# A gated linear recurrence with two dense blocks on one core: transfers issued some chain steps later, and a triangular solve laid out evenly over the chain

## The chip, the cores and the metric

The kernel runs on 1 core of one Trainium2 chip. The metric is the device time of one execution in microseconds (us); lower is better. The time before is a median of 1053.01 us over 2 runs (1050.19 and 1055.84).

## The reference, cut to what matters

Three blocks follow each other. The first, on which the change works, is a delta-rule recurrence over 768 positions with a 48 x 48 state for each of 4 x 8 (batch, head) pairs; two dense blocks in fp32 accuracy come after it.

```
k_n = k / (norm(k) + 1e-6)
for t in range(S):
    y[:, :, t] = q[:, :, t] @ state
    v_old = state^T k_n[t]
    state = state + beta[t] * outer(k_n[t], v[t] - v_old)
x = y as (4, 768, 384)
x = x + (gelu(x w_in)[u] * (w_sg layernorm(gelu(x w_in)[v]) + b)) w_out      # first dense block
x = u + relu(u w_ch1) w_ch2,   u = x + (relu(x^T w_tok1) w_tok2)^T           # second dense block
```

## The kernel before, in words

The recurrence (phase_a) is computed in chunks. The work is cut into 6 groups: 2 halves of the batch times 3 spans of 256 positions. For each group five things happen.

- **kk** (PE, lines 130 to 156): products of the keys (tile kq) with themselves, 4 units per group. ACT copies each unit into the staging tile gf, of which there is one buffer for two units; after the second and the fourth unit, six transfers within SBUF put gf into md and G (lines 152 and 153).
- **solve** (DVE, lines 158 to 195): a transpose of md into Li (line 161), a square root on ACT, eleven small steps of preparation, then 31 pairs, a product p (line 186) and a sum into T (line 188), each pair on the result of the last: the substitution. Then T is transposed into md (line 191) and into Tn (line 194). tload issues four transfers from md into tw (line 204).
- **merge** (PE, ACT; lines 209 to 242): 8 steps of products on tw, the first of them at line 216.
- **qk** (PE, DVE; lines 115 to 127): products of the keys with the queries (tile aq), 4 units; DVE masks each into aq (line 126).
- **chain** (PE, ACT; lines 248 to 303): 4 chunks of 4 steps (u, d0, y0, y1), 16 steps in all, which carry the state S from chunk to chunk through PSUM and the tiles yr. POOL multiplies the values v into yr (vput, line 247). The chains of the six groups run one after the other.

Every engine runs its instructions in the order in which the program emits them; nothing is reordered. The order is written by hand: while chain g emits its 16 steps, a table (ACT, one row per chain, one entry per step) says what is emitted behind each step: Q a unit of qk of group g+1, K a unit of kk of group g+3 (in chain 0 also of group 2), m a step of merge of group g+1, S n steps of the solve at hand, l the load of v, v a vput, z a memset of part of tw, c a piece of the conversion of the first dense block's weights (DVE lines 412 to 417, POOL, ACT), which goes on beside chains 1 and 2. A step S of the kind "pair" emits one pair. Between the two instructions of a pair a function (filler, line 317) may emit one step of the next group's solve, whenever that group's four units of kk have been emitted; it does so at a rate of 0.4 a call.

All loads go through SyncE's queue (SP), in the order of emission, as do the transfers within SBUF. A transfer that has to wait for the last reader of its buffer holds all that stand behind it. kq has two buffers (line 65, 2 transfers of 256 KB a load); its next load is emitted right behind the last product that reads the buffer. At the end of chain g the load of kn for group g+2 is emitted (line 83, 2 x 384 KB), and right behind it, as chain g+1 begins, those of bt for group g+3 (line 88, 16 KB) and of the queries for group g+2 (line 76, 2 x 512 KB). v is line 80.

In chain 5 the dense part begins beside the chain, and from there to the end PE multiplies.

Of the kernel before, what the change touches and what calls it, by code (L numbers as in the profile page):

```python
# [29 lines left out]
def phase_a(tc,I,xn,cfg,tail=None,beside=None,room=None):  # L30
    nc=cfg.get('wrap',lambda x:x)(tc.nc)
    es=ExitStack(); esE=ExitStack(); esP=ExitStack()
    with es:
# [80 lines left out]
        for par in range(2): nc.gpsimd.memset(AQs[1][T_[par],:,:,par].rearrange("p h b a c x -> p (h b) (a c x)"),0.0)  # L114
        def qk(g):
            for u in range(4):
# [6 lines left out]
                if u%2: load_kq()  # L123
# [4 lines left out]
        def kk(g):  # L128

            assert g<2 or merged[g-2]>=4 and loaded[g-2]  # L130
            for u in range(4):
# [7 lines left out]
                if u%2: load_kq()  # L139
# [6 lines left out]
                else:  # L146
                    if bb==0: gf=P1.tile([128,2,2,8,32],F32,name="gf")
                    nc.scalar.copy(gf[:,:,bb],gp.rearrange("p n (c i) -> p c n i",i=32))
                    if bb==1:
                        for r in range(4):  # L150
                            q=slice(32*r,32*r+32)
                            nc.sync.dma_start(md[q].rearrange("p (b h n) i -> p h b (n i)",b=2,h=2)[:,h],gf[q,r%2].rearrange("p b n i -> p b (n i)"))  # L152
                            if r%2==0: nc.sync.dma_start(G21[q].rearrange("p (b h n) i -> p h b (n i)",b=2,h=2)[:,h],gf[q,1].rearrange("p b n i -> p b (n i)"))
                done[g]+=1
                yield 'kk'
        done=[0]*6; merged=[0]*6; loaded=[0]*6; solved=[0]*6
# [160 lines left out]
        def filler():  # L317

            if len(run)>1 and done[run[1][0]]==4:
                acc[0]+=rate  # L320
                if acc[0]>=1: acc[0]-=1; next(run[1][1],None)
        def adv(n):
            for _ in range(n):
                if not run: return
# [10 lines left out]
        for ns in range(31):  # L335
            if ns==8: load_q(1); load_k(1)
# [4 lines left out]
        for k_ in range(4):  # L341
            many(s0,1)
            many(qks,1)
        many(ms,1); adv(1)
        many(ms,1)
        for k_ in range(6): many(ms,1); adv(1)
        vput(0,0)
        act=cfg['act']
        for g in range(6):
            if g+2<6: load_b(g+2)  # L350
            if g+1<6 and g>0: load_q(g+1)
# [4 lines left out]
            if g==5 and tail is not None:  # L356
                esP.close(); esE.close()
                fill=tail()
            for si,_ in enumerate(chain(g)):
                if fill is not None: next(fill,0)  # L360
                for a in act[min(g,5)][si].split():
# [7 lines left out]
                    if a=='l' and g<5: load_v(g+1)  # L369
# [3 lines left out]
            if g+2<6: load_k(g+2)  # L373
# [354 lines left out]
_mid=['m z S3','m S3','S3','S3','S3','Q S3','Q S3','Q S3','Q S3','l m S2','m S2','m S2','m K S2','m K S2','m K S2','K v S2']  # L728
_c=lambda row,at:[a+' c' if i in at else a for i,a in enumerate(row)]
ACT=[['S4 K','S4 K','S4 K','S4 K','S4','Q S4','Q S4','Q S4','Q S4','l m S2','m S2','m S2','m K S2','m K S2','m K S2','K v S2'],  # L730
# [34 lines left out]
```

## Time and profile before

| | |
|---|---|
| median of 2 runs | 1053.01 us |
| the profiled execution's own time | 1051.51 us |
| its span, first to last instruction | 1049.8 us |
| busy: PE, DVE, ACT, POOL | 872.0, 627.5, 350.7, 282.5 us |
| mean granted clock of PE | 0.904 of full speed |
| chains 0 to 4 (start of chain 0 to start of chain 5) | 76.2 to 366.6 us |

The profile is one execution. Its span is cut by stage: the first 76 us are the first loads, kk and the solve of group 0; then chains 0 to 4; then chain 5 beside the dense part. Group g's merge and chain need group g's solve, and a chain's middle needs the queries of the next group. A wait in brackets behind a row is idle time of that engine, put down to what came last.

### The profile page before, as it was taken

Reading aid. Unit: us, or ns where it says so; the run is one execution under the profiler, and the core shown is the slowest. Engines: PE = TensorE matmul, PEld = TensorE weight load, DVE = VectorE, ACT = ScalarE, POOL = GpSimd, SP = SyncE. Lnnn points to the kernel's source line nnn. Section 1 sums busy time; section 2 is a strip of 40 time slices with the busy share of each in tenths; the row PEclk is TensorE's granted clock in tenths of the full one; section 3 lists DMA queues with packets and bytes.
Section 4 is the critical chain, followed back from the end, with each engine's and each line's share of the span. In section 5 each row is a group of like instructions: output and inputs, shape, how many; then the busy total and the mean of one; then the engine's idle time right before and its main releaser. Section 6 shows DMA issues by size and latency. Waiting matters only on the chain.

```text
span 1049.8 us, 23037 instructions
## 1 busy us (share of the span) xinstructions
PE 872.0 (83%) x9644; PEld 827.4 (79%) x9644; DVE 627.5 (60%) x1294; ACT 350.7 (33%) x809; POOL 282.5 (27%) x358
## 2 busy tenths in 40 slices
PE   6375455755566998999999999789999999999998
PEld 4165455645556877899999999778889999999998
DVE  7977919969584247887494789786942222222222
ACT  2042233443326576444242343343422112112111
POOL 8110121645403143432232344482420000000000
PEclk7588678866778899999999999898999999999999
DMA  7633355573545143200000002222400000000000
GB/s 182 140 64 93 71 144 114 155 168 111 133 109 109 31 137 118 64 1 2 1 1 1 1 11 81 70 85 68 133 31 23 2 23 23 1 23 23 1 23 23
DMA packets 60024, 68.05 MB, mean 65 GB/s; under 512 B 30224, under 2 KB 37136, under 8 KB 59920
## 3 DMA queue, kind: packets, MB, share of 16 engines
q1 hardware_dynamic: 57808, 60.28, 21.8%
q0 software_dynamic: 2112, 6.29, 1.9%
q8 instruction: 76, 1.25, 0.5%
q14 instruction: 28, 0.23, 0.1%
HBM read 51.61 MB, written 7.86 MB: 57 GB/s over the span
## 4 chain that ended last, share of the span: by engine, by line
PE 60%; DVE 18%; ACT 7%; DMA 5%; issue 5%; SPq 4%; POOL 1%; DVEq 0%; ACTq 0%; POOLq 0%
PE ps L488 17%; PE ps L489 17%; PE ps L490 17%; DVE T L188 3%; DVE p L186 2%; DMA md<-gf 2%; DVE F L412 2%; DMA aq<-in_qt_dram 2%; DVE F L413 2%; PE gm L122 2%; PE gm L226 2%; SPq L152 2%; DVE aq L126 1%; PE gm L216 1%; PE ps L512 1%
## 5 line engine op out<-in xcount | busy, mean ns | idle before, releaser
L580 DVE SCALAR_TENSOR_TENSOR hlo<-ps,hh 128x384 fp32r<-128x384 f32 x96 | 53.5, 557 | 207.4 <-ACT hh L579 207.4
L579 ACT ACTIVATE hh<-ps 128x384 fp32r<-128x384 f32 x96 | 47.2, 492 | 228.2 <-PE ps L490 228.2
L488 PE MATMUL ps<-GU,SB 128*128 128x384 f32 x288 | 98.2, 341 | 0.0
L490 PE MATMUL ps<-GU,SB 128*128 128x384 f32 x288 | 98.0, 340 | 0.0
L489 PE MATMUL ps<-GU,SB 128*128 128x384 f32 x288 | 97.7, 339 | 0.0
L247 POOL TENSOR_TENSOR yr<-v,nn 64x192 f32<-64x192 f32 x96 | 50.9, 530 | 161.4 <-PE yp L255 84.8
L186 DVE TENSOR_TENSOR p<-Li,T 128x31 f32<-128x31 f32 (+15 forms) x186 | 71.2, 385 | 5.6
L122 PE MATMUL gm<-aq,kq 128*64 128x64 f32 x768 | 39.2, 270 | 41.0 <-issue 26.2
L188 DVE TENSOR_TENSOR T<-T,p 128x112 f32<-128x112 f32 (+15 forms) x186 | 69.4, 375 | 5.8
L122 PEld LDWEIGHTS gm<-aq,kq 128*64 128x64 f32 x768 | 35.7, 182 | 43.5 <-issue 35.6
L489 PE MATMUL ps<-SB,VHt 128*128 128x384 f32 x192 | 65.6, 342 | 2.3 <-POOL SB L390 2.3
L490 PE MATMUL ps<-VHt,hlo 128*128 128x384 f32 x192 | 65.3, 340 | 1.3 <-DVE hlo L580 1.3
L488 PE MATMUL ps<-SB,VHt 128*128 128x384 f32 x192 | 65.6, 341 | 0.0
L490 PE MATMUL ps<-SB,VHt 128*128 128x384 f32 x192 | 65.1, 339 | 0.0
L488 PE MATMUL ps<-VHt,hh 128*128 128x384 f32 x192 | 65.0, 338 | 0.0
L489 PE MATMUL ps<-VHt,hh 128*128 128x384 f32 x192 | 64.6, 337 | 0.0
L489 PEld LDWEIGHTS ps<-GU,SB 128*128 128x128 f32 x288 | 54.5, 189 | 0.7 <-DVE GU L505 0.7
L488 PEld LDWEIGHTS ps<-GU,SB 128*128 128x128 f32 x288 | 54.6, 190 | 0.5 <-DVE GU L505 0.5
L555 POOL TENSOR_TENSOR q<-q,u 128x384 f32<-128x384 f32 x32 | 36.9, 1156 | 66.4 <-DVE q L554 66.4
L490 PEld LDWEIGHTS ps<-GU,SB 128*128 128x128 f32 x288 | 54.4, 189 | 0.3 <-POOL SB L390 0.3
L488 PE MATMUL ps<-X,SA 128*128 128x384 f32 x144 | 50.0, 347 | 5.6 <-DVE xn L567 3.1
L265 PE MATMUL Sps<-yr,kn 128*48 128x48 f32 x704 | 31.6, 232 | 27.1 <-ACT yr L281 13.8
(157 smaller groups left out, 2313.9 us busy)
## 6 DMA issues: line engine op xcount, KB each, us to landing
kq<-in_kq_dram SPq DMA_DIRECT2D x48, 256.0 KB, 4.3
st<-in_ch_dram SPq DMA_DIRECT2D x36, 256.0 KB, 2.8
aq<-in_qt_dram SPq DMA_DIRECT2D x12, 512.0 KB, 8.0
v<-in_vn_dram SPq DMA_DIRECT2D x12, 384.0 KB, 5.6
kn<-in_kn_dram SPq DMA_DIRECT2D x12, 384.0 KB, 6.8
out_dram<-xn SPq DMA_DIRECT2D x24, 192.0 KB, 1.9
tw<-md SPq DMA_DIRECT2D x24, 128.0 KB, 3.7
st<-in_win_dram POOLq DMA_DIRECT2D x12, 256.0 KB, 4.0
```

The source lines that it names most:

```text
L122: nc.tensor.matmul(gp[T_[par],n,:],kq[F_,par,64*n:64*n+64],aq[F_,par,n//2,n%2,:],start=True,stop=True)
L152: nc.sync.dma_start(md[q].rearrange("p (b h n) i -> p h b (n i)",b=2,h=2)[:,h],gf[q,r%2].rearrange("p b n i -> p b (n i)"))
L186: nc.vector.tensor_tensor(p,Li[:,j,j+1:].unsqueeze(1).to_broadcast([128,w,n]),T[:,:w,j].unsqueeze(2).to_broadcast([128,w,n]),ALU.mult)
L188: nc.vector.tensor_tensor(T[:,:w,j+1:],T[:,:w,j+1:],p,ALU.add)
L247: n0=8*h+cc; nc.gpsimd.tensor_tensor(YRs[bb][gc%3][T_[par],:,par,:],VS[bb][T_[par],n0:n0+7:2,:],NNs[g%3][T_[par],16*bb+n0:16*bb+n0+7:2].un ...
L265: nc.tensor.matmul(Sps[bb][D_[par],pair,:],KNs[pb][F_,bb,par,c,pair,:],yr[F_,pair,par,:],start=(gc==0 and pair==0 and bb==0),stop=True,ski ...
L488: nc.tensor.matmul(ps,L[0],Rr[0],start=first,stop=False)
L489: nc.tensor.matmul(ps,L[0],Rr[1],start=False,stop=False)
L490: nc.tensor.matmul(ps,L[1],Rr[0],start=False,stop=last)
L555: nc.gpsimd.tensor_tensor(gt,gt,u2[:,d,t],ALU.mult)
L579: nc.scalar.activation(hi,ps,AF.Relu)
L580: nc.vector.scalar_tensor_tensor(lo,ps,0.0,R(hi),op0=ALU.max,op1=ALU.subtract)
```

## The change

Line numbers of the new kernel are some 10 higher (L152 is L161, L161 is L171, L186 is L196, L191 is L201, L126 is L134).

Three things are done. First, transfers are not emitted at once but put on a list (later) and emitted a number of chain steps on (tick counts them down at each step): kq 2 steps later, the md and G transfers 1 step later, bt and the queries at the first step of the chain, kn at the third (and only behind the queries), v 2 steps later. Second, the filler may begin a solve only 8 chain steps behind its last unit of kk. Third, the table gives each chain 38 solve steps, 2 or 3 at each chain step, which is one solve to a chain; chains 0 and 4 have 4 a step until the solve at hand is done. The second half of solve 5 so moves into chain 4, whose merge steps begin one step later.

```diff
+        wait=[]
+        def later(fn,n=cfg['late']):
+            wait.append([n,fn])
+        def tick():
+            for w in list(wait):
+                w[0]-=1
+                if w[0]<=0: wait.remove(w); w[1]()
...
-                if u%2: load_kq()
+                if u%2: later(load_kq)
...
                     if bb==1:
-                        for r in range(4):
-                            q=slice(32*r,32*r+32)
-                            nc.sync.dma_start(md[q]...,gf[q,r%2]...)
-                            if r%2==0: nc.sync.dma_start(G21[q]...,gf[q,1]...)
-                done[g]+=1
+                        def out(h=h,gf=gf,md=md,G21=G21):
+                            ...
+                        later(out,1)
+                done[g]+=1; dat[g]=step[0]
...
-            if len(run)>1 and done[run[1][0]]==4:
+            if len(run)>1 and done[run[1][0]]==4 and step[0]>=dat[run[1][0]]+cfg['far']:
...
-                if not run: return
+                if not run or done[run[0][0]]<4: return
...
         for g in range(6):
-            if g+2<6: load_b(g+2)
-            if g+1<6 and g>0: load_q(g+1)
+            if g+2<6: later(lambda g=g:load_b(g+2),1)
+            if g+1<6 and g>0: later(lambda g=g:load_q(g+1),1)
+            if g and g+1<6: later(lambda g=g:load_k(g+1),3)
...
+                while wait: tick()
...
             for si,_ in enumerate(chain(g)):
+                step[0]+=1; tick()
...
-                    if a=='l' and g<5: load_v(g+1)
+                    if a=='l' and g<5: later(lambda g=g:load_v(g+1),2)
...
-            if g+2<6: load_k(g+2)
...
-_mid=['m z S3','m S3','S3','S3','S3','Q S3','Q S3','Q S3','Q S3','l m S2','m S2','m S2','m K S2','m K S2','m K S2','K v S2']
+_st=[2,3,2,3,2,2,3,2,2,3,2,2,3,2,2,3]
+_s=dict(m=(0,1,9,10,11,12,13,14),Q=(5,6,7,8),l=(9,),v=(15,))
...
-CFG={...,'rate':.4,'act':ACT}
+CFG={...,'rate':.4,'late':2,'far':8,'act':ACT}
```

How the instructions of two engines move, each time without the row numbers. First SyncE's queue in chain 1, around the first of the two sets of six md and G transfers of a group (md_142 and G_128 are those of group 4; kq_110 and kq_111 are the two key buffers). Before:

```order
L65 DMA kq_110<-in_kq_dram 64x2x512 x2
L152 DMA md_142<-gf 32x2x256
L153 DMA G_128<-gf 32x2x256
L152 DMA md_142<-gf 32x2x256 x2
L153 DMA G_128<-gf 32x2x256
L152 DMA md_142<-gf 32x2x256
L65 DMA kq_111<-in_kq_dram 64x2x512 x2
```

and after:

```order
L161 DMA md_142<-gf 32x2x256
L162 DMA G_128<-gf 32x2x256
L161 DMA md_142<-gf 32x2x256 x2
L162 DMA G_128<-gf 32x2x256
L161 DMA md_142<-gf 32x2x256
L65 DMA kq_110<-in_kq_dram 64x2x512 x2
```

The load of kq_110 stood ahead of the first set of six transfers and now stands behind it, so that it is what the second set follows; the load of kq_111 moved on likewise, behind the second set.

SyncE's queue a little later, where chain 2 starts, from the last two of the second set on (kn_101, bt_122, aq_97 are the loads for the next groups, tw_99 takes the result of solve 3). Before:

```order
L153 DMA G_128<-gf 32x2x256
L152 DMA md_142<-gf 32x2x256
L83 DMA kn_101<-in_kn_dram 64x2x768 x2
L88 DMA bt_122<-in_bt_dram 128x32
L76 DMA aq_97<-in_qt_dram 64x4x512 x2
L204 DMA tw_99<-md_143 32x32x32 x4
```

and after:

```order
L162 DMA G_128<-gf 32x2x256
L161 DMA md_142<-gf 32x2x256
L88 DMA bt_122<-in_bt_dram 128x32
L76 DMA aq_97<-in_qt_dram 64x4x512 x2
L65 DMA kq_111<-in_kq_dram 64x2x512 x2
L83 DMA kn_101<-in_kn_dram 64x2x768 x2
L214 DMA tw_99<-md_143 32x32x32 x4
```

The queries (aq) moved ahead of kn, and the second load of kq went between the two.

DVE at the end of solve 3 (T_147, p_154; Li_144 and md_142 belong to solve 4, md_143 and Tn_149 to solve 3; F is the weight conversion, aq_97 the masking of the next group's queries). Before:

```order
L186 TENSOR_TENSOR p_154<-Li_145,T_147 128x60
L188 TENSOR_TENSOR T_147<-T_147,p_154 128x30x2
L186 TENSOR_TENSOR p_154<-Li_145,T_147 128x31
L161 STREAM_TRANSPOSE Li_144<-md_142 128x1024
L188 TENSOR_TENSOR T_147<-T_147,p_154 128x31
L191 STREAM_TRANSPOSE md_143<-T_147 128x32x32
L194 STREAM_TRANSPOSE Tn_149<-T_147 128x32x32
L169 TENSOR_SCALAR rc<-sh 128x32
```

and after:

```order
L196 TENSOR_TENSOR p_154<-Li_145,T_147 128x60
L198 TENSOR_TENSOR T_147<-T_147,p_154 128x30x2
L196 TENSOR_TENSOR p_154<-Li_145,T_147 128x31
L198 TENSOR_TENSOR T_147<-T_147,p_154 128x31
L201 STREAM_TRANSPOSE md_143<-T_147 128x32x32
L134 TENSOR_TENSOR aq_97<-gm,mask 64x512 x2
L204 STREAM_TRANSPOSE Tn_149<-T_147 128x32x32
L171 STREAM_TRANSPOSE Li_144<-md_142 128x1024
L134 TENSOR_TENSOR aq_97<-gm,mask 64x512 x2
L425 TENSOR_SCALAR F<-st 128x256 x2
L426 SCALAR_TENSOR_TENSOR F<-st,F 128x256 x2
L427 SCALAR_TENSOR_TENSOR F<-st,F 128x256 x2
```

The transpose into Li_144 stood ahead of the last T of solve 3 and ahead of the transpose into md_143; now it stands behind both transposes of solve 3. The end of solve 3, which stood at the start of chain 2, now stands between the maskings of chain 2's steps 6 and 8.

## Rows read from the trace of the kernel before

**Rows 1.** The busy time of each engine in 13 stretches of the run, us from the span's start, from chain 0's start to chain 5's start. Columns: stretch, its length; then for PE, PEld, DVE, ACT and POOL the busy us (and the number of instructions); the granted clock of PE; the mean busy share of the DMA engines; GB/s moved.

```profile
76.17:120.04 43.87, 20.06 (x490) 19.20 (x485) 35.61 (x88) 10.95 (x31) 2.07 (x4) 0.76 0.29 66
120.04:148.75 28.71, 21.06 (x645) 19.90 (x647) 12.00 (x28) 13.39 (x29) 11.77 (x19) 0.80 0.55 137
148.75:163.41 14.66, 8.21 (x162) 7.60 (x158) 8.79 (x23) 6.44 (x19) 1.88 (x2) 0.60 0.69 155
163.41:183.65 20.24, 8.73 (x222) 8.34 (x223) 19.29 (x51) 3.89 (x13) 2.64 (x5) 0.83 0.43 97
183.65:211.70 28.05, 19.91 (x647) 18.62 (x649) 26.12 (x57) 14.83 (x34) 17.56 (x31) 0.81 0.49 145
211.70:229.99 18.29, 8.64 (x162) 8.32 (x158) 9.69 (x17) 7.52 (x21) 7.00 (x13) 0.63 0.86 195
229.99:251.87 21.88, 9.64 (x223) 9.28 (x224) 20.76 (x53) 3.65 (x11) 9.48 (x17) 0.62 0.45 119
251.87:276.36 24.49, 19.13 (x631) 18.12 (x632) 21.46 (x44) 12.95 (x27) 16.93 (x32) 0.85 0.43 129
276.36:296.21 19.85, 8.30 (x144) 7.45 (x140) 6.93 (x21) 6.77 (x19) 1.64 (x4) 0.59 0.70 141
296.21:312.75 16.54, 9.98 (x222) 9.70 (x223) 15.45 (x35) 2.87 (x9) 1.06 (x2) 0.77 0.19 59
312.75:327.60 14.85, 13.38 (x478) 12.51 (x479) 13.92 (x30) 10.25 (x23) 5.69 (x9) 0.89 0.22 65
327.60:349.49 21.89, 13.66 (x343) 12.99 (x341) 3.73 (x5) 8.47 (x24) 4.29 (x9) 0.77 0.64 128
349.49:366.60 17.11, 16.40 (x626) 15.64 (x625) 2.75 (x4) 13.45 (x31) 2.28 (x5) 1.00 0.09 28
```

**Rows 2.** Waits over the whole run: who waited for whom, us in total, times, the longest.

```profile
DVE Li L161 <- DMA md<-gf: 43.5, 4, 21.2
...
ACT gf L148 <- DMA md<-gf: 36.8, 5, 8.7
```

**Rows 3.** DVE in order of time at the start of chain 2. Columns here and in the groups of single instructions below: start us, us, engine, line, operation, out<-in, shapes, count, and in brackets the idle time before it with what ended it. The last two rows are the first of solve 4's preparation and its first product.

```profile
220.75 1.90 DVE L161 STREAM_TRANSPOSE Li<-md 128x1024 f32<-128x1024 f32 x1 [8.31 <-DMA md<-gf]
...
222.78 2.09 DVE L191 STREAM_TRANSPOSE md<-T 128x1024 f32<-128x1024 f32 x1
...
226.51 0.17 DVE L169 TENSOR_SCALAR rc<-sh 128x32 f32<-128x32 f32 x1
...
229.86 0.19 DVE L186 TENSOR_TENSOR p<-Li,T 128x31 f32<-128x31 f32 x1
```

**Rows 4.** SyncE's queue at the same place: issues of transfers.

```profile
197.09 1.31 SPq L65 DMA_DIRECT2D kq<-in_kq_dram  x2
198.45 1.19 SPq L152 DMA_DIRECT2D md<-gf  x1
...
216.99 1.24 SPq L83 DMA_DIRECT2D kn<-in_kn_dram  x2
...
218.91 1.24 SPq L76 DMA_DIRECT2D aq<-in_qt_dram  x2
```

**Rows 5.** DVE in chain 0: the transpose into Li of solve 2, and the md transpose of solve 1.

```profile
95.87 1.91 DVE L161 STREAM_TRANSPOSE Li<-md 128x1024 f32<-128x1024 f32 x1 [6.11 <-DMA md<-gf]
...
112.81 1.97 DVE L191 STREAM_TRANSPOSE md<-T 128x1024 f32<-128x1024 f32 x1
```

**Rows 6.** PE: the first merge product of group 1 in chain 0, and 32 query products of chain 2.

```profile
120.04 1.92 PE L216 MATMUL gm<-tw,G 128*32 128x32 f32 x62 [1.89 <-DMA tw<-md]
...
240.95 1.97 PE L122 MATMUL gm<-aq,kq 128*64 128x64 f32 x32 [7.59 <-issue]
```

**Rows 7.** ACT: the copy into gf that is the first of a group's second half, in chains 0, 1 and 2.

```profile
146.27 0.58 ACT L148 COPY gf<-gm 128x512 f32<-128x512 f32 x1 [7.88 <-DMA md<-gf]
...
208.57 0.59 ACT L148 COPY gf<-gm 128x512 f32<-128x512 f32 x1 [8.72 <-DMA md<-gf]
...
274.52 0.58 ACT L148 COPY gf<-gm 128x512 f32<-128x512 f32 x1 [6.28 <-DMA md<-gf]
```

**Rows 8.** The chain that ended last, in order of time: three pieces that are transfers under way. Columns: start us (the issue), us until landed, what.

```profile
85.49 2.05 DMA md<-gf
...
155.20 8.07 DMA aq<-in_qt_dram
...
202.28 6.20 DMA md<-gf
```

**Rows 9.** DVE, single instructions: the first of a weight conversion (line 412) and the product that follows the conversion; a T beside work of POOL; a masking; the first p of solve 5, a T of the same shape without work of POOL, and the solve's last T.

```profile
231.28 0.49 DVE L412 TENSOR_SCALAR F<-st 128x256 int32<-128x256 int32 x2
...
233.69 0.27 DVE L186 TENSOR_TENSOR p<-Li,T 128x112 f32<-128x112 f32 x1
...
236.80 0.77 DVE L188 TENSOR_TENSOR T<-T,p 128x175 f32<-128x175 f32 x1
...
239.45 1.39 DVE L126 TENSOR_TENSOR aq<-gm,mask 64x512 f32<-64x512 f32 x2
...
294.04 0.19 DVE L186 TENSOR_TENSOR p<-Li,T 128x31 f32<-128x31 f32 x1
...
320.13 0.34 DVE L188 TENSOR_TENSOR T<-T,p 128x175 f32<-128x175 f32 x1
...
324.34 0.21 DVE L188 TENSOR_TENSOR T<-T,p 128x31 f32<-128x31 f32 x1
```

## What I predict, and why

> **What bounds the kernel now.** I read the trace from the end. Of the span of 1049.8 us only the first third can move: from 366.6 us on chain 5 and the dense layers run, which the change does not touch. So I cut the stretch from chain 0's start (76.17) to chain 5's start (366.60) into stages, one row each [rows 1]. Three kinds recur. A runs from a group's last gf copy to the first product that needs the next queries (tile aq). B runs from there to the first merge product, line 216. C runs from that to the next group's last gf copy. The 13 rows add to 290.4 us, and in them DVE is busy for 196.5, PE for 177.1. Nothing is full over the whole; the engines take turns.
>
> Then the waits say who holds whom [rows 2]. DVE stands 43.5 us, four times, at the transpose into Li (line 161) for the transfers md<-gf. ACT stands 36.8 us because gf has one buffer and its next copy needs those transfers landed. Chain 2's start shows it in single rows [rows 3]: the Li transpose of solve 4 begins at 220.75 after 8.31 us of idleness, and the final md transpose of solve 3, ready since the last product p, comes behind it at 222.78. A helper that should fill gaps put the next solve's first step ahead of the last steps of the current one. SP shows why the transfer is late [rows 4]: two kq loads (256 KB each) go at 197.09, ahead of the md transfers at 198.45; and kn (2 x 384 KB) at 216.99 goes ahead of the queries at 218.91.
>
> **Part 1: the filler no longer starts a solve early.** In the order after, Li stands behind the md transpose of the solve before. In chain 0 the md transpose begins at 112.81 [rows 5]. Ahead of it go away: the wait 6.11, the transpose 1.90, the preparation of solve 2 (226.51 to 229.86 for solve 4 [rows 3], so 3.35) and some 1.0 of its first pairs, 12.4 in all. I give 1.5 back, since the masking products on DVE then wait for PE. The transfer to tw and its landing stay: from the transpose's end (114.8) to the merge at 120.04 [rows 6] are 5.2. So the first stage goes from 43.87 to 33.0.
>
> **Part 2: md<-gf before kq.** In C the second gf copy waits 7.88, 8.72 and 6.28 us [rows 7]. With SP free, six issues take 4.1 us (198.45 is the first, 202.28 the last, which is under way from then [rows 4, 8]); from the last one's issue to the landing it took 2.05 at best and 6.20 with kq under way [rows 8]. From the copy's end to the last landing that is some 5.7, of which ACT works 1.9 on merge copies (in between now too), so it waits 3.8. The saving is 4.1, 4.9 and 2.5: C becomes 24.6, 23.1 and 22.0. Bounds: if transfers still land as at 202.28, nothing is saved; if ACT waits for nothing, 7.9, 8.7 and 6.3.
>
> **Part 3: kn behind the queries.** After: md 4.1, bt 0.65, then aq, first issue 4.75 after the gf copy. Two transfers of 512 KB at the 195 GB/s with a 0.86 share [rows 1], so some 215 at full share, take 4.9, and 2.05 is added as for the smallest landing: A = 11.6. Before, it was 14.66, 18.29 and 19.85. I let the queries set A in each chain, since the rows of A end at the product that waited for them. The observed landing of 8.07 with kn ahead [rows 8] is the other end: A = 13.4. The Trainium skill, DMA: Bandwidth & Descriptors, section "Anatomy of one DMA", gives some 2.0 us plus the bytes at 436 GB/s; by it A would be 9.2 and the total 7 us lower. It speaks of transfers issued by GpSimd, these go through SP, and no row here shows such a rate.
>
> **Part 4: the solve ends just in time.** This is what the change pays. Before, solves 2 to 5 were complete one half chain before their merge. Now the md transpose stands at step 6 and the merge at step 9, so B is a chain of its own: products 2.0 at the low clock [rows 6], mask 1.4 [rows 9], two pairs 1.2, mask 1.4, two pairs 0.9, transpose 2.05, tw 5.2: 14.2. (A pair is a p and a T; 31 of them take 294.04 to 324.55 less four maskings, 24.9, or 0.80 each [rows 9], the last ones least.) In chains 1 and 2 a conversion of weights (231.28 to 233.69, 2.4, taken as 2.7 with its neighbour's start [rows 9]) lies inside: 16.9. Before, B was 20.24, 21.88 and 16.54, because three pairs, not two, stood between the maskings. Chain 4 loses its free ride: half of solve 5 now lies in it. From the md transpose of solve 4, DVE still does 1.9 + 1.9 + three maskings 4.3 + 3.35 + 24.9 + 2.05 = 38.4; of these the 14.9 of the stage before pass first, so the row of 21.89 becomes 23.5. The merge of group 5 begins one step later, and the tail's first transposes wait for its last copy: 17.11 becomes 18.3.
>
> Priced at nothing: kq, issued two steps later, is read four steps on, some 12 us in C; if that cover went, PE would wait one landing each. kn is used in step 13, 11 steps later. v is used at step 15; it now stands behind two kq, whose products end before. bt was waited for once and is ahead of its reader by a chain half. What queues behind the md issue on SP is bt, aq, kq, kn, tw; tw is issued some 15 us after the rest, so the queue is empty by then.
>
> **The sum.** After, in order: 33.0 + 24.6 + (11.6 + 16.9 + 23.1) + (11.6 + 16.9 + 22.0) + (11.6 + 14.2 + 14.9) + 23.5 + 18.3 = 242.2. Is DVE able to follow? From one md transpose to the next it works 1.9 + 1.9 + four maskings 5.7 + 3.35 + 24.9 + 2.05 = 39.8, plus 2.7 for each conversion: 42.5, 50.6, 42.5, 38.4. The path through SP, ACT and PE takes 53.1, 51.6, 47.7 and 38.4. The second and fourth have no slack, and a T beside work of POOL took 0.77 where alone it takes 0.34 [rows 9]. I add 4.5: six such hits and some waiting. So 246.7 instead of 290.4: 43.7 gone. The profiled execution took 1051.5 us with its ends, so 1007.8; the median of the two runs shown is 1.5 higher, so the forecast is 1009. What is late next is the queries' landing (A) and then the solve in front of its own merge (B).
>
> **Rivals.**
> (1) The transfers land as late as now, since SP's queue and not its order holds them: A stays near 14.7 to 18 and C as it is. Then only the first stage (10.9) and B (3.3 + 5.0 + 2.3) give, less 2.8 at the end and the 4.5, and a little of A: some 18, so 1035. For it: landings of 8.07 in rows. Against: the DMA share in C is 0.43 to 0.55, so there is room.
> (2) Slower: DVE cannot follow. One mechanism, in the pairs of every solve, which are now spread next to POOL's multiplications into yr: each p and T takes the contended price, +0.43, or 0.86 a pair. 124 pairs would add 107 us to DVE; 16 of slack and 4.5 are paid already, so 1009 + 86 = 1095. It makes the kernel slower than before once a pair costs 0.52 more on average. Against: POOL is busy for 84.3 of the 290.4 us, the sum of its column in [rows 1], and a collision costs no more than POOL's own time. The Trainium skill, SBUF — State Buffer, section "Who interferes with whom", says that a DVE instruction with two SBUF inputs contends with a GpSimd one that reads SBUF, which is the pair and the multiplication here; the row of 0.77, beside a POOL subtraction, agrees.
> (3) The solves are all that remains: A lands early and DVE sets every cycle. Then the 190.8 of the four cycles become 174, and the total 990.
>
> **How the numbers follow.** Forecast 0.70, rival 1 0.17, rival 2 0.05, rival 3 0.08. The forecast's own ends: A 9.9 to 13.4 (three times, -5 and +5), C with nothing saved (+11.5) or no wait (-11), the addition 0 to 9 (-4.5 and +4.5): not all at once, so 994 to 1030, which ends short of the middle of rivals 1 and 3; I take 988 to 1034, which holds rival 3 and part of rival 1. A measurement of this kernel can tell some 2%, 21 us, from no change. Faster by more: the forecast, rival 3 and a third of rival 1, 0.84. Within 2%: the rest of rival 1, 0.11. Slower: 0.05.
>
> **What would show it.** No DVE wait at Li for md<-gf above 2 us; last gf copy to first query product 10 to 13 us; merge 14 to 17 after that product, released by tw<-md; G to G 50 to 54 us in chains 1 and 2 (63.0 and 64.7 now); chain 5 starting near 323. It is wrong if aq is issued more than 6 us after the gf copy, if C keeps its waits of 6 to 9 us, or if a pair takes more than 0.95 (0.80 now).

## The result, and the profile after

The kernel takes 1017.05 us (median of 2 runs, 1016.73 and 1017.37): 0.9658 of the time before, 95% interval 0.9546 to 0.9771. I forecast 1009 with a range of 988 to 1034. The gain is 36 us where I worked out 44. The profiled execution took 1016.73 us, and its span is 1015.0.

The same 13 stretches as in [rows 1], from chain 0's start to chain 5's start (columns as there):

```profile
76.76:111.24 34.48, 17.94 (x489) 17.08 (x484) 31.47 (x68) 10.85 (x31) 2.17 (x4) 0.84 0.31 69
111.24:137.94 26.70, 20.39 (x634) 19.25 (x636) 24.56 (x64) 12.81 (x28) 11.78 (x19) 0.82 0.56 145
137.94:151.04 13.10, 7.60 (x172) 7.12 (x170) 0.00 (x0) 7.68 (x22) 0.00 (x0) 0.76 0.62 143
151.04:168.94 17.90, 9.09 (x224) 8.63 (x225) 15.42 (x26) 3.48 (x11) 7.74 (x14) 0.79 0.64 144
168.94:193.35 24.41, 19.25 (x634) 18.10 (x636) 23.20 (x58) 14.12 (x33) 18.34 (x30) 0.92 0.59 178
193.35:206.76 13.41, 7.42 (x172) 6.82 (x169) 12.72 (x30) 8.35 (x24) 7.36 (x14) 0.75 0.73 181
206.76:224.66 17.90, 9.16 (x224) 8.72 (x225) 16.70 (x31) 3.27 (x10) 8.87 (x17) 0.69 0.65 172
224.66:247.59 22.93, 19.46 (x622) 18.41 (x624) 21.58 (x53) 12.21 (x27) 14.46 (x25) 0.87 0.51 139
247.59:261.24 13.65, 7.04 (x152) 6.50 (x149) 8.86 (x23) 6.97 (x20) 1.15 (x2) 0.75 0.67 153
261.24:275.60 14.36, 8.45 (x225) 8.12 (x225) 11.88 (x18) 2.40 (x8) 1.01 (x2) 0.86 0.54 101
275.60:291.00 15.40, 14.85 (x481) 13.91 (x483) 14.22 (x40) 10.81 (x25) 6.05 (x9) 0.81 0.47 127
291.00:316.71 25.71, 16.47 (x404) 15.49 (x399) 23.43 (x46) 9.39 (x27) 5.04 (x10) 0.78 0.52 105
316.71:332.72 16.01, 15.39 (x564) 14.72 (x563) 0.00 (x0) 12.71 (x29) 2.45 (x7) 0.93 0.09 36
```

They add to 256.0 us; before they added to 290.4. Outside them nothing moved: 1016.7 - 256.0 = 760.7 and 1051.5 - 290.4 = 761.1. DVE is busy for 204.0 of them, where it was 196.5: less idling, not less work. In the third stretch it does nothing at all. One thing differs between the two tables: in [rows 1] a stretch A starts at the end of the last gf copy, here at its start, 0.6 us earlier. From the copy's end A is 12.5, 12.8 and 13.0 us here.

The waits that answer to [rows 2] (who waited for whom: us over the run, times, longest):

```profile
ACT gf L156 <- DMA md<-gf: 29.8, 5, 7.3
...
DVE aq L134 <- PE gm L130: 24.3, 6, 15.2
...
PE gm L226 <- DMA tw<-md: 22.5, 7, 6.9
...
PE gm L130 <- DMA aq<-in_qt_dram: 17.9, 7, 4.8
```

There is no row any more for DVE at Li; 43.5 us of it are gone. ACT still waits for md<-gf, 29.8 us instead of 36.8. DVE's wait at the masking stayed, 24.3 us where it was 20.8. PE's waits for tw and for the queries grew, from 8.9 and 5.4 us to 22.5 and 17.9. The place of [rows 3], DVE in time:

```profile
217.26 2.09 DVE L201 STREAM_TRANSPOSE md<-T 128x1024 f32<-128x1024 f32 x1
...
220.80 1.91 DVE L204 STREAM_TRANSPOSE Tn<-T 128x1024 f32<-128x1024 f32 x1
222.57 1.82 DVE L171 STREAM_TRANSPOSE Li<-md 128x1024 f32<-128x1024 f32 x1
```

The transpose into Li stands behind both transposes of the solve before, and none of them has a wait in brackets. SyncE's queue at the place of [rows 4]:

```profile
193.96 0.64 SPq L161 DMA_DIRECT2D md<-gf  x1
...
199.38 1.27 SPq L76 DMA_DIRECT2D aq<-in_qt_dram  x2
200.73 1.30 SPq L65 DMA_DIRECT2D kq<-in_kq_dram  x2
202.09 1.24 SPq L83 DMA_DIRECT2D kn<-in_kn_dram  x2
```

The last gf copy of this group began at 193.35; the first aq issue follows 6.0 us later, ahead of kq and kn. The waits at gf that answer to [rows 7], ACT in chains 0, 1 and 2:

```profile
136.04 0.58 ACT L156 COPY gf<-gm 128x512 f32<-128x512 f32 x1 [7.27 <-DMA md<-gf]
...
191.44 0.58 ACT L156 COPY gf<-gm 128x512 f32<-128x512 f32 x1 [5.45 <-DMA md<-gf]
...
246.37 0.58 ACT L156 COPY gf<-gm 128x512 f32<-128x512 f32 x1 [4.98 <-DMA md<-gf]
```

What answers to [rows 8], pieces of the chain that ended last (issue, us to landing):

```profile
130.73 5.14 DMA md<-gf
...
144.37 6.63 DMA aq<-in_qt_dram
...
187.63 3.56 DMA md<-gf
...
200.06 6.66 DMA aq<-in_qt_dram
...
243.26 2.80 DMA md<-gf
...
254.35 6.84 DMA aq<-in_qt_dram
```

And DVE's first masking in chains 1, 2 and 3 with the idle time before it:

```profile
153.05 1.39 DVE L134 TENSOR_TENSOR aq<-gm,mask 64x512 f32<-64x512 f32 x2 [15.22 <-PE gm L130]
...
208.77 1.39 DVE L134 TENSOR_TENSOR aq<-gm,mask 64x512 f32<-64x512 f32 x2 [0.60 <-PE gm L130]
...
263.25 1.39 DVE L134 TENSOR_TENSOR aq<-gm,mask 64x512 f32<-64x512 f32 x2 [6.04 <-PE gm L130]
```

### The profile page after: what moved, and what is told of

Read it like the earlier page. It is cut to its first block, busy times and chain, and to the rows that moved or that the text cites. A ratio compares the mean times of both kernels' runs of the same rounds, so it can differ in the third digit from the quotient of the medians.

```text
span 1015.0 us, 23038 instructions
## 1 busy us (share of the span) xinstructions
PE 862.6 (85%) x9644; PEld 820.0 (81%) x9644; DVE 636.6 (63%) x1294; ACT 350.6 (35%) x809; POOL 284.2 (28%) x358
## 3 DMA queue, kind: packets, MB, share of 16 engines
q1 hardware_dynamic: 57808, 60.28, 22.5%
## 4 chain that ended last, share of the span: by engine, by line
PE 64%; DVE 20%; DMA 5%; ACT 4%; issue 3%; SPq 2%; POOL 2%; ACTq 0%; DVEq 0%; POOLq 0%
PE ps L502 18%; PE ps L501 17%; PE ps L503 17%; DVE p L196 3%; DVE T L198 3%; DMA aq<-in_qt_dram 2%; DVE F L425 2%; DVE aq L134 2%; DVE F L426 2%; PE gm L130 2%; PE gm L236 1%; PE gm L226 1%; PE gm L146 1%; PE yp L265 1%; PE gm L248 1%
## 5 line engine op out<-in xcount | busy, mean ns | idle before, releaser
L196 DVE TENSOR_TENSOR p<-Li,T 128x31 f32<-128x31 f32 (+15 forms) x186 | 74.9, 403 | 6.0
L198 DVE TENSOR_TENSOR T<-T,p 128x31 f32<-128x31 f32 (+15 forms) x186 | 72.5, 390 | 6.4
L130 PE MATMUL gm<-aq,kq 128*64 128x64 f32 x768 | 37.7, 258 | 37.5 <-DMA aq<-in_qt_dram 17.9
L568 POOL TENSOR_TENSOR q<-q,u 128x384 f32<-128x384 f32 x32 | 36.8, 1154 | 66.5 <-DVE q L567 66.5
L289 PE MATMUL ck<-yr,tw 128*64 128x48 f32 x768 | 34.6, 232 | 17.4 <-ACT yr L277 14.9
## 6 DMA issues: line engine op xcount, KB each, us to landing
kq<-in_kq_dram SPq DMA_DIRECT2D x48, 256.0 KB, 4.8
st<-in_ch_dram SPq DMA_DIRECT2D x36, 256.0 KB, 2.8
st<-in_win_dram POOLq DMA_DIRECT2D x12, 256.0 KB, 3.7
```

Source lines behind the costliest of these rows:

```text
L130: nc.tensor.matmul(gp[T_[par],n,:],kq[F_,par,64*n:64*n+64],aq[F_,par,n//2,n%2,:],start=True,stop=True)
L196: nc.vector.tensor_tensor(p,Li[:,j,j+1:].unsqueeze(1).to_broadcast([128,w,n]),T[:,:w,j].unsqueeze(2).to_broadcast([128,w,n]),ALU.mult)
L198: nc.vector.tensor_tensor(T[:,:w,j+1:],T[:,:w,j+1:],p,ALU.add)
L289: nc.tensor.matmul(u2[T_[par],pair,:],tw[F_,par,16*bb+8*h+2*pair+cc,:],yr[F_,pair,par,:],start=True,stop=True)
L568: nc.gpsimd.tensor_tensor(gt,gt,u2[:,d,t],ALU.mult)
```

## Experiments

One table for all runs. The stages are read as in the rows of the kernel after: A from the start of the last gf copy to the query products that need the whole of aq (its second load too), B to the merge products, C to the start of the next last gf copy, for chains 1 to 3 (C: 0 to 2). The row of the kernel before is read in the same way, so its A is 0.6 us longer and its C shorter than in [rows 1]. "chains" is chain 0's start to chain 5's start. Stages are from one profiled execution each, the times are medians, the ratios are to the kernel before. Two runs whose intervals overlap cannot be told apart by their times.

| kernel | us | ratio, 95% | A | B | C | chains |
|---|---|---|---|---|---|---|
| before | 1053.0 | | 15.2, 18.9, 20.5 | 20.2, 21.9, 16.5 | 28.1, 27.5, 23.9 | 290.4 |
| after | 1017.1 | 0.955 to 0.977 | 13.1, 13.4, 13.7 | 17.9, 17.9, 14.4 | 26.7, 24.4, 22.9 | 256.0 |
| e1 order alone | 1032.6 | 0.976 to 0.983 | 16.4, 17.5, 16.3 | 17.7, 18.0, 14.4 | 29.6, 26.1, 23.9 | 271.6 |
| e2 transfers, old table | 1026.7 | 0.971 to 0.978 | 13.9, 15.1, 13.1 | 18.4, 19.1, 13.8 | 22.8, 28.9, 23.2 | 262.9 |
| e3 aq first | 1003.3 | 0.949 to 0.960 | 7.2, 8.2, 7.6 | 17.3, 21.7, 13.8 | 25.6, 25.6, 23.6 | 241.2 |
| e4 two gf | 1014.4 | 0.959 to 0.966 | 19.1, 18.7, 16.6 | 17.5, 18.1, 14.4 | 19.4, 20.4, 19.0 | 253.8 |
| e5 kn ahead | 1025.5 | 0.971 to 0.978 | 15.9, 16.3, 16.2 | 17.6, 18.0, 14.5 | 25.8, 24.7, 23.5 | 263.0 |
| e6 = e3 + lead | 1001.7 | 0.948 to 0.955 | 9.3, 9.3, 6.5 | 16.0, 21.9, 16.1 | 24.4, 25.7, 22.0 | 239.2 |
| e7 = e3, less conversion | 1005.3 | 0.951 to 0.960 | 7.6, 10.7, 7.7 | 15.4, 16.8, 13.5 | 25.7, 25.3, 23.0 | 236.3 |
| e8 kq behind | 1022.6 | 0.968 to 0.975 | 15.6, 15.6, 16.1 | 17.7, 18.1, 14.8 | 23.9, 24.3, 23.8 | 260.9 |
| e9 = e6 + two gf | 1003.9 | 0.948 to 0.957 | 14.2, 14.1, 12.0 | 16.8, 22.1, 14.4 | 20.3, 20.8, 18.3 | 241.2 |
| e10 = e3, masks on POOL in chains 3, 4 | 1007.6 | 0.952 to 0.960 | | | | 243.0 |
| e11 = e6, masks on POOL in chains 1 to 4 | 1013.4 | 0.958 to 0.967 | | | | 253.1 |
| e12 = e3, no vput | 994.3 | 0.942 to 0.948 | | | | 237.1 |

### The two halves of the change, each alone

e1 undoes the transfers (`later` calls at once, kn at the chain's end); e2 undoes the table, but not all of the order, since the filler still pauses, for 2 chain steps:

```diff
 e1:          def later(fn,n=cfg['late']):
-            wait.append([n,fn])
+            fn()
 e2: the ACT table of before, and
-'far':8
+'far':2
```

> The new table and the later start of each solve alone: every load and transfer is emitted at once, as in the kernel before, kn at the end of the chain. My theory (the two halves of the change add up, each in its own stages): the first stage keeps its 9.4 us of gain and the B stages (first query product to first merge product) their 8.4, chain 4 keeps its loss of 3.8, the last stage its 1.1; the A stages (last gf copy to first query product) stay at 14.7, 18.3 and 19.9 us and the C stages (merge to last gf copy) at 28.7, 28.1 and 24.5: 1053 - 15 = 1038 us. Rival 1 (the order alone does it, the transfers are hidden anyway): 1017 to 1022. Rival 2 (with a solve that ends just in time, late transfers are no longer covered and cost more than they did): 1045 or more.

> The later transfers alone: the old table, and the filler may begin a solve 2 chain steps behind its last unit of kk (by then its md transfers have been emitted), nearly as before. My theory: the A stages give 12.7 us and the C stages 7.2, the first stage and B nothing: 1053 - 20 = 1033 us. Rival 1 (the transposes into Li still stand ahead of the end of the solve at hand and wait, so DVE gives much of it back): 1043 to 1053. Rival 2 (transfers do all): 1017 to 1022.

Measured: 1032.6 and 1026.7. Each won more than I had worked out for it and less than a rival that gives it everything. Alone they win 2.0% and 2.5%, together 3.4%; in the chains 18.8 and 27.5 us, together 34.4. So some 12 us are won by either. (By the medians alone that is not clear of the noise, since the kernel after ran only twice.) Where the two overlap shows at Li in e2:

```profile
DVE Li L171 <- DMA md<-gf: 19.2, 4, 13.4
...
203.47 2.11 DVE L201 STREAM_TRANSPOSE md<-T 128x1024 f32<-128x1024 f32 x1
...
210.01 1.91 DVE L171 STREAM_TRANSPOSE Li<-md 128x1024 f32<-128x1024 f32 x1 [2.64 <-DMA md<-gf]
```

DVE's wait at Li fell from 43.5 [rows 2] to 19.2 us. I had given this wait to the order alone, and mostly it belongs there. Even the short pause of the filler lets DVE come to Li later: it has more pairs to do first (chain 0), Li stands behind the md transpose of the solve before (chain 2, the two single rows), or that solve ends later (chain 3). The waits there fell from 6.1, 8.3 and 7.9 us to 0.4, 2.6 and 2.9. In chain 1 the wait fell from 21.2 to 13.4, since the last gf copy came 9.3 us earlier (138.89 instead of 148.17); from that copy's start to the last landing of md the transfers take no less than before, 8.1 us instead of 5.9. So e2 is not the transfers alone, and how much of the 12 us is the piece of the order that it keeps is not shown.

In e1 the wait at gf stays at 35.6 us over the run, and the A stages of chains 1 and 2 stay within 1.4 us of the kernel before. That of chain 3 falls by 4.2: before, four transfers of tw (280.74 to 282.96) stood ahead of kn (284.18) and the queries, and with the new order they come later. So a part of A belongs to the order as well.

### A: where the queries stand in SP's queue

e5 puts kn ahead of bt and aq again; e3 issues aq as the chain begins, ahead of the second md set:

```diff
 e5:
-            if g and g+1<6: later(lambda g=g:load_k(g+1),3)
+            if g and g+1<6: later(lambda g=g:load_k(g+1),1)    # ahead of load_b, load_q
 e3:
-            if g+1<6 and g>0: later(lambda g=g:load_q(g+1),1)
+            if g+1<6 and g>0: load_q(g+1)
```

> The new kernel with one thing undone: the load of kn (2 x 384 KB) goes ahead of bt and the queries again, at the first step of the chain. My theory (a load's landing is set by the bytes that stand ahead of it in the queue): 768 KB at 215 GB/s are 3.6 us, so A is 3.6 us longer in chains 1 to 3, of which chain 2 loses as much too: 1017 + 10 = 1027 us. Rival 1 (kn's bytes share the engines with aq wherever it stands, order is nothing): 1017 to 1019. Rival 2 (only the issue of 1.3 us counts): 1021.

> The new kernel, but the queries (aq) are emitted as the chain begins, ahead of the second set of md and G transfers (before: behind it and bt). My theory (A is the place of aq in SP's queue, 4.4 us of issues, plus its landing): aq is issued some 5 us earlier, A becomes 9 us in chains 1 and 3, where DVE waits 15.2 and 6.0 us for the query products; in chain 2 DVE waits only 0.6, so it sets the pace and little is won: 1017 - 10 = 1007 us. Rival 1 (aq is slow because it shares the DMA engines, so it lands at the same time): 1015 to 1018. Rival 2 (every A is worth its length): 1017 - 14 = 1003.

e5 took 1025.5 (forecast 1027): against the kernel after, A grew by 2.8, 2.9 and 2.6 us, somewhat under the 3.6 of kn's bytes and twice its issue of 1.3. The bytes ahead of a load count, not its issue alone. e3 took 1003.3, the time of my second rival; its stages say why it is not that rival's reason. (The intervals of e3 and of the kernel after overlap a little, since the latter ran only twice; e3's four runs, 1001.2 to 1010.8 us, lie below both of its runs.) Three A with the B behind each, e3's windows (columns as in [rows 1]):

```profile
137.47:144.66 7.19, 7.09 (x171) 6.90 (x168) 0.68 (x3) 6.01 (x17) 0.00 (x0) 0.74 1.06 223
144.66:161.93 17.27, 8.03 (x234) 7.20 (x228) 15.33 (x26) 5.04 (x17) 7.75 (x14) 0.89 0.72 170
187.55:195.75 8.20, 7.61 (x170) 7.42 (x168) 7.86 (x20) 6.67 (x19) 3.61 (x7) 0.70 0.97 253
195.75:217.47 21.72, 9.41 (x234) 8.81 (x228) 20.86 (x38) 5.48 (x17) 12.93 (x24) 0.74 0.75 172
241.03:247.49 6.46, 6.26 (x154) 6.05 (x151) 5.98 (x15) 5.92 (x17) 1.25 (x2) 0.80 0.99 221
247.49:262.40 14.91, 7.52 (x234) 6.97 (x228) 14.20 (x25) 3.42 (x12) 1.01 (x2) 0.94 0.72 141
```

The fifth row ends at the first two query products, which need only the first load of aq; the others follow at 248.62, so that A, read like the rest, is 7.6 and the B behind it 13.8. A fell by 5.9, 5.2 and 6.1, further than I had worked out. In chain 2 the B behind it grew from 17.9 to 21.7: there DVE was full (20.86 of 21.72 us) and took 3.8 of 5.2 back, as my theory had it. Of rival 1 a part is true: in chain 1 the second load of aq was issued 10.5 us earlier than in the kernel after (133.91 instead of 144.37), but landed only 6.1 us earlier (144.91 instead of 151.00).

In the A stages the DMA engines are at a share of 0.97 to 1.06 and move 221 to 253 GB/s. This is the rate of all transfers together, and my 215 was near it. The Trainium skill, DMA: Bandwidth & Descriptors, section "Anatomy of one DMA", gives 2.0 us plus the bytes at 436 GB/s for a transfer issued by GpSimd; my estimate from that is 4.4 us for the two loads of aq as one transfer. The trace of after has 6.6 to 6.8 us behind the second issue, on SP's queue and with the loads of kq and kn issued right behind, so for these loads the trace differs from the page's fit.

### C: the wait at gf

e4 has two gf buffers; e8 puts kq's load behind the second md set; e9 is e6 (below) with two gf buffers:

```diff
 e4, e9 (and one buffer of Tn, to make room):
-                    if bb==0: gf=P1.tile([128,2,2,8,32],F32,name="gf")
+                    if bb==0: gf=P1.tile([128,2,2,8,32],F32,name="gf",bufs=2)
 e8:
-                if u%2: later(load_kq)
+                if u%2 and (u==3 or g<3): later(load_kq)
...
                         later(out,1)
+                        if g>2 and h: later(load_kq,1)
```

> The new kernel with two buffers of gf (room for it from a single buffer of Tn, whose next writer comes behind its last reader in any case). The copies into gf, which waited 7.3, 5.5 and 5.0 us in chains 0, 1 and 2, wait no more. My theory (behind C0 DVE stands idle for 15 us at the masking, so what C0 loses is won; in chains 1 and 2 DVE is busy for 95% of C and gives 1.2 and 1.3 at most): 1017 - 8 = 1009 us. Rival 1 (each wait is worth its length): 999. Rival 2 (the waits are only moved, to the products of the merge or to DVE): 1015 to 1018.

> The new kernel, but the kq load that stood right behind the first set of md and G transfers of a group goes behind the second set (and so ahead of bt and the queries). My theory (the landing of md behind its last issue, 5.1, 3.6 and 2.8 us in chains 0, 1 and 2, is long because kq's 512 KB follow at once and share the engines): landings of 2.1 us, the waits of ACT at gf fall from 7.3, 5.5 and 5.0 to 4.3, 4.0 and 4.3, C is 3.0, 1.5 and 0.7 us shorter; but the queries stand behind kq's 512 KB and A is 2.4 longer each time: 1017 + 2 = 1019 us. Rival 1 (other traffic, the weight pieces of POOL's queue, makes md slow): the gf waits stay at 7.3, 5.5, 5.0 and the time is 1024. Rival 2 (A is not lengthened since kq and aq share the same stretch): 1012.

> The queries first and 7 solve steps earlier (1002 us), with two buffers of gf beside (and one of Tn), so that no copy into gf waits. My theory (in that kernel DVE is busy nearly without a gap from chain 1's first masking on, so the 5.7, 4.4 and 5.1 us of ACT's waits are worth only what DVE still idles): 1002 - 3 = 999 us. Rival 1 (each wait is worth its length): 987. Rival 2 (md, kq and aq now stand in one burst and the queries land later, as in the run with two gf buffers alone): 1002 to 1006.

e4: all gf waits for md<-gf are gone and C is 7.3, 4.0 and 3.9 us shorter, but A is 6.0, 5.3 and 2.9 longer; 2.6 us are left of it, which cannot be told from nothing, nearest to rival 2. PE in chain 1 shows what took the wait's place:

```profile
147.23 0.45 PE L131 MATMUL gm<-aq,kq 128*64 128x64 f32 x2 [9.93 <-DMA aq<-in_qt_dram]
149.64 0.59 PE L131 MATMUL gm<-aq,kq 128*64 128x64 f32 x6 [1.96 <-DMA aq<-in_qt_dram]
```

All transfers now start in one burst (md, kq, md, bt, aq, beside the weight pieces), and aq is nearly as late as it was: its second load is issued 4.5 us earlier than in the kernel after (139.88 instead of 144.37) and lands only 1.4 us earlier (149.59 instead of 151.00). e9 (1003.9) says the same of the faster kernel: C is shorter and A longer than in e6, and the time is that of e6. Its median lies in rival 2's range, though its interval (some 998 to 1007) holds my 999 too; rival 1's 987 is out. e8 took 1022.6, between my 1019 and rival 1: A grew by 2.5, 2.2 and 2.4, as worked out, but the gf waits are 5.8, 5.0 and 5.4 where I put 4.3, 4.0 and 4.3, since md's landing behind its last issue hardly fell (the chain of waits of e8):

```profile
128.43 3.96 DMA md<-gf
...
186.69 3.19 DMA md<-gf
...
244.74 3.23 DMA md<-gf
```

5.14, 3.56 and 2.80 became 3.96, 3.19 and 3.23, so kq is not what makes these landings long. Nor can the 1.2 us of chain 0 be given to kq alone: two weight pieces of POOL's queue were issued around that transfer in the kernel after (130.42 and 131.18, the transfer at 130.73) and behind it in e8 (128.47 and 129.23, the transfer at 128.43). Rival 1, which puts it on these pieces, is not settled; no run takes them away, and in chain 2 of e8 the last landing took 3.23 us with the last of them issued at 206.08. A load behind a set is not enough to make it slow either: in the kernel after, the second set of each group has bt and aq right behind it and its last transfer landed in 2.60, 2.03 and 2.05 us. What sets the 2.0 here and the 3 to 5 there stays open.

### DVE: what the solves cost

All on e3 (e11 on e6). e6 moves 7 solve steps ahead of chain 1's maskings, e7 cuts the conversion's DVE work, e10 and e11 move maskings to ACT and POOL, e12 leaves out POOL's multiplications:

```diff
 e6: chain 1's row
-_row(_st,K=(12,13,14,15),c=(2,5,8,11),...)
+_row([4,4,4,4,3]+_st[5:],K=(12,13,14,15),c=(2,5,8,11),...)
 e7: three of the four DVE lines of conv
-            for j in m: nc.vector...
+            for j in (m if out is None else ()): nc.vector...
 e10 (g>3), e11 (g>1, and e6's row):
-                    nc.vector.tensor_tensor(aq...,gp[rr],mask...,ALU.mult)
+                    nc.scalar.copy(ao,gp[rr]); nc.gpsimd.tensor_tensor(ao,ao,mk,ALU.mult)
 e12: vput
+                    if gc==0: nc.gpsimd.tensor_tensor(YRs...)
```

> The queries issued first (as in the run that measured 1003), and 7 more solve steps in the first five steps of chain 1, so that the end of solve 2 is emitted ahead of the maskings and every later solve runs 7 steps ahead. My theory (with the queries first DVE sets everything from chain 1 on except one idle stretch of 7.9 us ahead of the first masking of chain 1; it is filled): 1003 - 7 = 996 us. Rival 1 (the solve that ends just in time costs B its tw transfer, so taking it off the path of B gives more, 4 us in each of three chains): 991. Rival 2 (the transpose into Li now waits for md again and the maskings queue behind it): 1003 to 1008.

> The queries issued first (1003 us), and three of the four DVE instructions of each piece of the weight conversion beside chains 1 and 2 left out (so the weights are not converted): 2.0 us of DVE work for each of 6 pieces, 12 us. My theory (DVE is what sets the pace from chain 1's first masking on): most of it is won, 1003 - 10 = 993 us. Rival (PE, ACT and the transfers set the pace, DVE only looks full because its instructions stretch beside POOL): 1000 to 1004.

> The queries first (1003 us), and the masking of the query products of groups 4 and 5, emitted in chains 3 and 4, taken off DVE: ACT copies the product into aq, POOL multiplies it with the mask there. It takes 8 maskings of 1.39 us, 11 us, off DVE where POOL is nearly idle, and frees the product's PSUM buffer as soon as ACT has copied. My theory (in these two chains DVE's work is the path): 1003 - 8 = 995 us. Rival 1 (of work taken off DVE only 4 parts in 10 come out, as 4.9 of some 12 us did when the conversion was cut): 999. Rival 2 (POOL's multiplications slow p and T by as much): 1002 to 1006.

> The queries first and 7 solve steps earlier (1002 us), and the masking of groups 2 to 5 taken off DVE in the same way: 16 maskings, 22 us of DVE's work. My theory (DVE's work is the path from chain 1 on, about half of the 22 us is taken back where POOL now works beside p and T, since a T took 0.77 us beside POOL and 0.34 alone): 1002 - 11 = 991 us. Rival 1 (nothing is taken back): 980. Rival 2 (POOL, which also splits the weights and writes v, becomes the path, the masked queries come late): 1002 to 1010.

> The queries first (1003 us), and POOL's multiplications of v into yr left out, but for the first chunk of each half (so the state gets no new values): some 29 us of POOL's work between chain 1's first masking and chain 4's last, while DVE does the pairs of the solves. My theory (in that stretch DVE has no idle time to speak of and pays for each collision; when the maskings went to POOL, 20 us more of POOL's work in chains 3 and 4 made p and T slower by 62 ns each, 6 us in all, so 3 parts in 10): 9 us of DVE's work go, 1003 - 8 = 995 us, and p and T fall from 401 and 397 ns to 370. Rival 1 (the slow p and T are slow for another reason, a bound of the instruction itself): p and T stay at 400, the time at 1001 to 1005. Rival 2 (every us of POOL's work is a us of DVE's, as one T of 0.77 where alone it takes 0.34 would have it): p and T at 300, 980 us.

e6 won 2 us of 7 in the chains (1001.7; its interval overlaps e3's, the two cannot be told apart). Ahead of chain 1's first masking DVE now idles 2.2 us, at Li and put down to bt, instead of 7.9. But its queue reaches the maskings of chains 2 and 3 late, and PE waits for them with the third query unit:

```profile
207.57 1.73 PE L130 MATMUL gm<-aq,kq 128*64 128x64 f32 x27 [6.92 <-DVE aq L134]
...
257.03 1.23 PE L130 MATMUL gm<-aq,kq 128*64 128x64 f32 x18 [5.97 <-DVE aq L134]
```

e7 missed: the time did not fall (1005.3, not to be told from e3). Of the 13.3 us that the three instructions took in e3, 4.9 came out of the chains (241.2 to 236.3); the rest turned into waits of DVE, which between 76 and 302 us grew from 8.7 to 16.8 us: at the maskings (11.0) and, new, for ACT's square and POOL ahead of the conversion's last step (5.8). The dense part behind the chains took 6.3 us more in that profile, the largest piece a wait of PE of 5.3 us for DVE; its cause is open. e10 (1007.6) cannot be told from e3, so no gain is shown; e11 (1013.4) was slower than e6, somewhat above its second rival. In e11 it is DVE's pairs that are late, more than POOL's queue. Beside POOL's six maskings from 296.44 on, six p and T in a row take 1.27 to 1.30 us each, about a masking's length, whatever their shape:

```profile
296.44 7.94 POOL L136 TENSOR_TENSOR aq<-aq,mask 64x512 f32<-64x512 f32 x6
...
300.55 1.30 DVE L201 TENSOR_TENSOR T<-T,p 128x112 f32<-128x112 f32 x1
```

In the same solve a T of this shape took 0.28 us at 274.17. Over solve 5 a p and a T take 548 and 554 ns where e6 has 399 and 386; its md transpose comes at 306.80, and PE waits 13.8 us for tw behind it. At line 292 PE waits 7.9 us in all for POOL's yr.

What POOL's work costs DVE the pairs of the other runs show as well, DVE's p and T from 76 to 330 us, first e3, then e10, then e12 (busy us, mean ns):

```profile
L196 DVE TENSOR_TENSOR p<-Li,T 128x87 f32<-128x87 f32 (+15 forms) x153 | 61.3, 401 | 5.0
L198 DVE TENSOR_TENSOR T<-T,p 128x31 f32<-128x31 f32 (+15 forms) x154 | 61.2, 397 | 5.3
```

```profile
L201 DVE TENSOR_TENSOR T<-T,p 128x112 f32<-128x112 f32 (+15 forms) x152 | 63.8, 419 | 5.2
L199 DVE TENSOR_TENSOR p<-Li,T 128x31 f32<-128x31 f32 (+15 forms) x151 | 63.6, 421 | 4.9
```

```profile
L196 DVE TENSOR_TENSOR p<-Li,T 128x156 f32<-128x156 f32 (+15 forms) x150 | 55.7, 371 | 4.9
L198 DVE TENSOR_TENSOR T<-T,p 128x31 f32<-128x31 f32 (+15 forms) x151 | 54.5, 361 | 5.2
```

The pairs take 401 and 397 ns in e3, 421 and 419 with the maskings of two chains on POOL, 371 and 361 with the multiplications of v taken off POOL. On average a pair pays 66 ns, 8%, for POOL's multiplications. Single rows show how: of the first solve in e3, the six products that run beside POOL's multiplications (28.5 to 35.4 us, 0.57 us each) take 0.57 to 0.58 us, be they of 60 or of 175 elements; with POOL done by 30.8 in e12, those of 112 to 175 take 0.27 to 0.34. The Trainium skill, SBUF — State Buffer, section "Who interferes with whom", says that a DVE instruction with two inputs in SBUF contends with a GpSimd instruction that reads SBUF; these rows agree. e12's 994.3 is my number (995), but not for my reason alone: of the 10 us that 153 pairs save, 4.1 came out of the chains and the rest went into DVE's waits (8.7 to 15.2 us) as in e7; 4.0 more came ahead of and behind the chains (2.1 of them in the first solve, whose last p begins at 52.51 instead of 54.59).

## Why the prediction was right, and where its sizes were off

- **The mechanism held.** Only the stages moved, and what lies outside them stayed; Li's wait is gone; the queries' landing sets A in chains 1 and 3; B is a chain of masks, pairs, transpose and tw; chain 4 pays.
- **Part 1, first stage: 33.0, measured 34.5.** The md transpose came at 104.02, 27.3 us into the stage instead of 36.6, so 9.4 are won, not 10.9: the wait of 6.1 and 4.3 us of DVE's work (28.6 to 24.4), less 0.9 of waiting at the first masking. I had taken 6.3 for the work; the pairs up to there cost 20.3 us with 54 instructions where 59 cost 20.4. From the transpose's end to the merge (111.24) there are again 5.2 us [rows 6].
- **Part 2, C: 24.6, 23.1, 22.0; measured 26.7, 24.4, 22.9.** This is the weak part. The wait at gf came out at 7.3, 5.5 and 5.0 where I put 3.8, so it fell by 5.2 us in all and not by 11.5. The term that failed is the landing: I took 2.05, the smallest in [rows 8], for the last of six in a row. It was itself the last of such a set (issued from 81.14 to 85.49 in the kernel before), so it was of the right kind, but one of the short ones; here the last lands 2.8 to 5.1 us behind its issue. I also put the long one, 6.20, down to kq under way. But the kq loads ahead of it had landed by 201.95, before it was issued at 202.28, and the short one had a kq load right behind it too (86.18). e8 shows that kq is a small part of the wait.
- **Part 3, A: 11.6; measured 12.5, 12.8 and 13.0 from the copy's end, as I had counted.** aq's first issue came 5.2 to 5.5 us behind that end (I put 4.75), and its second load landed 7.3 to 7.5 us behind the first issue (I put 6.95): both terms near, both short. That aq's place in the queue rules A is shown by e3 and e5 from both sides, but not one for one (e3, e4).
- **Part 4, B: 16.9, 16.9, 14.2; measured 17.9, 17.9, 14.4.** Near. e6 adds that the end of the solve is not alone on this path: with it out of the way B stays at 16.0, 21.9 and 16.1, because the maskings stand in the same queue. Chain 4 was 2.2 us longer than I said (25.7), the last stage 2.3 shorter (16.0); that they add to 41.7 against 41.8 is luck.
- **The sum.** Against 242.2 without the allowance, the terms missed by 1.5 (first), 3.6 (A) and 6.1 (C, both from the copy's end), 2.2 (B), 0.5 (before chain 4) and nothing in the last two together: 13.8 (rounded), of which I had allowed 4.5. So every term but the last was somewhat short; the two largest misses, C and A, are the ones that I had priced with the smallest landing in view.
- **"DVE follows".** Right for this kernel, with slack in another place than I put it: DVE waited 15.2 and 6.0 us at the maskings of chains 1 and 3 and 0.6 in chain 2, so A set the pace in two of three chains.
- **The signs I had named.** No wait at Li: so. A of 10 to 13 and B of 14 to 17: A up to 13.0 from the copy's end, B up to 0.9 over. G to G of 50 to 54: 55.4 and 54.2. Chain 5 near 323: 332.7. Two signs of being wrong were near or there: aq issued more than 6 us behind the gf copy (5.2 to 5.5 from its end, 5.7 to 6.1 from its start), and C's waits of 6 to 9 us, where chain 0's 7.3 lies and the others' 5.5 and 5.0 do not. A's and C's sizes were the weak part.
- **The rivals.** Rival 1's price was near: 1035, and e1, whose transfers go as before, took 1032.6. Rival 2's mechanism is real but small: p and T rose from 385 and 375 ns before (over the whole run) to 403 and 390, so a pair costs 0.03 us more where 0.52 would have undone the gain. Rival 3 is where e3 and e6 arrive, at 1003 and 1002 instead of 990: between md transposes they take 50.0, 55.4, 45.3 and 39.5 us (e3: 104.47, 154.44, 209.81, 255.08, 294.53), with 7.9 idle in the first, so DVE's work is 182 us and not the 174 I had put. The 66 ns a pair that e12 shows are 8 us in 124 pairs, the same size; that they are the same thing is an inference.

So in e3 DVE looks like the bound and is one only stretch by stretch: of the work that e7 and e12 take off it, six parts in ten come back as waits of DVE, most of them for PE and ACT.

## What to carry to other kernels

When two changes work on the same wait, their gains need not add: run each alone before you split a gain between them, and look in the trace whether the run leaves out what it is said to leave out (e2 still moved Li). In a queue of loads that is worked off in order, look for the one load that somebody waits for and issue it before the transfers that nobody needs yet; here that was worth some 14 us on top of the 36 of the change itself. Price a transfer by its landings at that place in several cycles, not by the fastest that you find, and do not name a cause for a long one before you have looked what else was under way.

## What I had not expected of the hardware

- Sets of six transfers of 64 KB within SBUF, issued 0.6 to 0.7 us apart with few gaps, landed their last 2.8 to 5.1 us behind its issue for the first set of a group, and 2.0 to 2.6 us for the second (the kernel after, chains 0 to 2). The cause is open.
- With the DMA engines full (share 0.97 to 1.06) all transfers of this kernel together moved 221 to 253 GB/s; taking a buffer wait away (e4) then only moved the wait to the next load.
- Work that is moved from DVE to POOL comes back in part: a p or T that ran beside a masking of POOL took 1.27 to 1.30 us in e11, the masking's own length, where its shape alone takes 0.28 to 0.30; in e10 POOL's 16 maskings (1.27 us each) went with 20 ns more on every p and 22 on every T between 76 and 330 us.
